# Attention in twelve batches of score chunks, and the root of the first norm in one turn

## The chip, the cores and the metric

The kernel runs on one core of a Trainium2 chip. The engines are TensorE (PE in the profile; PEld is its loading of weights), VectorE (DVE), ScalarE (ACT), GpSimd (POOL, unused here) and SyncE (SP), which issues nearly all transfers. The metric is the device time of one execution in microseconds (us), lower is better. Each engine executes its instructions in the order in which the program gives them, and waits on semaphores for the others.

## The reference

Three stages follow each other: attention with a sigmoid in place of the softmax (2 batches, 12 heads, 448 positions, 64 columns a head), a gated MLP with an RMS norm ahead of it (896 tokens, 768 to 1536 to 768), and an MLP with a SiLU (768 to 2048 to 768).

```python
scores = scale * np.matmul(q, k.transpose(0, 1, 3, 2)) - np.log(S)
attn = 1.0 / (1.0 + np.exp(-scores))
x = np.matmul(attn, v)          # then heads side by side: 896 x 768
rms = np.sqrt(np.mean(x * x, axis=-1, keepdims=True) + 1e-06)
xn = x / rms * rms_g
g = xn @ w_gate
x = (g * (1.0 / (1.0 + np.exp(-g))) * (xn @ w_val)) @ w_out
h = x @ w_in
return (h * (1.0 / (1.0 + np.exp(-h)))) @ w_out2
```

## The kernel before

**Pairs and chunks.** Attention works on 12 pairs of heads: pairs 0 to 5 are batch 0, pairs 6 to 11 batch 1. The 448 keys of a pair are three full chunks of 128 (c = 0, 1, 2) and a rest of 64. The rests of two neighbouring pairs, i and i + 1 with i even, form one chunk (i, 3), written (i, KC) in the code. So two pairs have seven chunks, and all have 42.

**Scores (`scores`, L403).** A full chunk is 6 matmuls in 64x128 tiles, for two heads side by side: k and q are split into a high part (fp32r) and a low rest, and three products are added. Their operand `ks` is made by `prep` on VectorE: a cast (L379) and a subtraction (L267); there are three buffers. A short chunk is 4 matmuls of unsplit fp32 in 64x64 tiles (8 records in the profile, since an fp32 matmul leaves two). Scores land in one of three PSUM tiles (`scp`, bufs=3), and ScalarE's sigmoid (L413) empties it into `a`.

**Attends (`attend`, L431).** A full chunk is 2 fp32 matmuls in 128x64 tiles (4 records), a short one 4 in 64x64 tiles (8 records), summed over a pair's chunks in a bank `av`, of which there are two (`avp`, bufs=2): pair 9 takes the bank of pair 7. `collect` copies a finished pair out of `av` into `xr` on VectorE (L448), which frees the bank. The square of the copy is made by ScalarE (L587), or, for pairs listed in `SQUARED`, by VectorE (L454); `add_square` adds it to the sum `acc` of its batch on VectorE (L467). The squares of pairs 7 to 10 share one buffer (tag s1, one deep).

**Turns.** `SIZES` cuts the list of chunks into batches. A turn issues the scores of one batch (full chunks first, the short one last) and then the attends of the batch before. When the scores of chunk (i, 0) are issued, `prep(i + 1)` and the loads of pair i + 3 are issued ahead of them. `PLAN` says what each turn issues at its end: `w` a step of the preparation of weights (merge of a slab, L288, casts, rests), `n` a step of `norm_first`; `EARLY` gives turn 9 one more `n` behind its scores.

**The norm of batch 0 (`norm_first`).** Its steps: split the sum of squares; two matmuls with ones that sum it over partitions (`ms0`, L472); first guess of the root (L482, L483) and a square on ScalarE (L486); a Newton step (L489, L490) and another square (L529); the last step (L493 to L495), which gives `r0`; then `normed`: for the x tiles in the order 0, 2, 4, 1, 3, 5, two at a time, scale on VectorE (L507), cast on ScalarE (L264, `high`) and rest on VectorE (L267, `low`). The first product behind attention (`g0`, L872) reads them in that order, six tiles and three matmuls each, of which the second needs the rest. The sums for batch 1 (into `v1_1`) and the product `g1` follow it; the banks for these overlay `av`, so `g1` also waits for the last `collect`.

**Behind attention** a planner (`Plan`) orders all work by fixed costs and due times. Those costs are not touched by the change.

Of the kernel before, what the change touches and what calls it, by code (L numbers as in the profile page):

```python
# [23 lines left out]
KC = S // P  # L24
# [3 lines left out]
HALF = 3 * P  # L28
NT = B * S
EPS = 1e-6  # L30
SIZES = [2, 2, 3] + [4, 3] * 5
DIRECT = ((0, 0),)
WOVEN = ((0, 1), (0, 2))
IDLE = 9
FIRST = (0, 1)
AFTER = {2: 1, 3: 1, 4: 2, 5: 4, 6: 4, 7: 5}
AWAY = (4,)
SQUARED = (5, 9)
ALIGNED = 4
LAG = {"A": 0.0481, "D": 0.081, "P": 0.165, "S": 4.4}  # L40
LOAD, LOAD_TILE = 2.8, 0.45
HOP = {"A": 0.516, "D": 0.3833, "S": 0.4}
# [10 lines left out]
LOADED = (6, 7)  # L53
LANDED = {7: 8.0}
LONG = 288
PLAN = ",,,www,wwwww,wwwww,wwww,wwww,nw,nn,n,wn,wnwn,w".split(",")
EARLY = {9: "n"}
LOADS = (0, 2)
RING = 9
# [5 lines left out]
class Job:  # L65


    def __init__(self, eng, cost, fn, deps, take, need):
# [3 lines left out]
        self.due, self.ready, self.left = 1e9, 0.0, 0  # L72
        self.lag = LAG[eng]
        for d in self.deps:
# [129 lines left out]
def tile_attention_two_mlps(  # L204
# [53 lines left out]
    def load_next():  # L258
        s = order.pop(0)
        place(s)  # L260
        load(s)
# [4 lines left out]
    def low(dst, src, hi):  # L266
        nc.vector.tensor_tensor(dst, src, hi.bitcast(F32), ALU.subtract)  # L267
# [60 lines left out]
    def step():  # L328
        do = next(steps, None)
        if do:  # L330
            do()
# [11 lines left out]
    with ExitStack() as actx:  # L343
# [9 lines left out]
        def pair_tile(i):  # L353
            kq[i] = ap.tile([P, 2, S], F32, tag="kq", name=f"kq{i}", bufs=6)

        def load_pair(i):
            b, hp = pairs[i]
            if i not in kq:
                pair_tile(i)
            if i:  # L360
                nc.sync.dma_start(kq[i], kqd[b, hp])
            else:
                nc.scalar.dma_start(kq[i][:, 1], kqd[b, hp, :, 1])
                for part in (slice(0, P), slice(P, S)):
                    nc.sync.dma_start(kq[i][:, 0, part], kqd[b, hp, :, 0, part])

        def load_v(i):
            vr[i] = ap.tile([P, KC + 1, 2, D], F32, tag="vr", name=f"vr{i}", bufs=5)
            n = KC if i % 2 else KC + 1
            if i == 0:  # L370
                nc.vector.memset(vr[i], 0.0)
            nc.sync.dma_start(vr[i][:, :n], vd[pairs[i]][:, :n])

        def prep(i):

            raw = kq[i]
            ks[i] = kst = ap.tile([P, 2, 2, S], F32R, tag="ks", name=f"ks{i}", bufs=3)
            if i:
                nc.vector.tensor_copy(kst[:, 0], raw)  # L379
                for part in (slice(0, 1), slice(1, 2)) if i == 1 else (slice(0, 2),):  # L380
                    low(kst[:, 1, part], raw[:, part], kst[:, 0, part])
            else:
                (hk, hq), (lk, lq) = ([kst[:, j, n] for n in range(2)] for j in range(2))
                tail = slice(P, S)
                nc.scalar.activation(hq, raw[:, 1], AF.Copy)
                nc.vector.tensor_copy(hk[:, tail], raw[:, 0, tail])
                low(lk[:, tail], raw[:, 0, tail], hk[:, tail])
                low(lq, raw[:, 1], hq)
# [27 lines left out]
        begun = {}  # L416

        def attend(i, c):

            a = att.pop((i, c))  # L420
            if c < KC:
                parts = [(i, slice(0, P))]
            else:
                parts = [(i + e, slice(e * KR, (e + 1) * KR)) for e in range(2)]
            for n, rows in parts:
                begun[n] = begun.get(n, 0) + 1
                if begun[n] == 1:
                    av[n] = avp.tile([P, 512], F32, tag="av", name=f"av{n}")
            for h in range(2):
                for n, rows in parts:  # L430
                    nc.tensor.matmul(  # L431
                        av[n][h * D : (h + 1) * D, :S],
                        vr[i][rows, c, h, :],
                        a[rows, h, :],
                        start=(begun[n] == 1),
                        stop=(begun[n] == KC + 1),
                        skip_group_check=True,
                    )
            return [n for n, rows in parts if begun[n] == KC + 1]

        def collect(i, copy_=True):

            b, hp = pairs[i]
            ps = av.pop(i)[:, :S]
            which, home_ = ("s1" if copy_ else "s3", sqs) if hp else ("s0", acc)
            xi = xr[hp // 2][:, b, hp % 2]
            if i < n - 2:
                nc.vector.tensor_copy(xi, ps)  # L448
            while added:
                add_square(added.pop(0))  # L450
            sq = home_[i if hp else b] = sp.tile([P, S], F32, tag=which, name=f"{which}{i}")
            if i < n - 2:
                if i in SQUARED:
                    nc.vector.tensor_tensor(sq, xi, xi, ALU.mult)  # L454
                else:
                    later.append((i, sq, xi))
            else:
                nc.scalar.activation(sq, ps, AF.Square)
                if copy_:
                    nc.vector.tensor_copy(xi, ps)  # L460
            return lambda: nc.vector.tensor_copy(xi, ps)

        def add_square(i):

            b, hp = pairs[i]
            if hp:
                nc.vector.tensor_tensor(acc[b], acc[b], sqs.pop(i), ALU.add)  # L467
# [6 lines left out]
        def split_sum(b, parts):  # L474

            high(parts[:, 0], acc[b])
            low(parts[:, 1], acc[b], parts[:, 0])
# [57 lines left out]
        n = len(pairs)  # L535
# [17 lines left out]
        load_v(2)  # L553
        nc.sync.dma_start(g_sb, gd)
        prep(0)
        turn_, ready, later, added, woven = 0, [], [], [], []
        chunks = []
        for i in range(0, n, 2):
            chunks += [(i, c) for c in range(KC + 1)] + [(i + 1, c) for c in range(KC)]
        batches = [[chunks.pop(0) for _ in range(n)] for n in SIZES]  # L560
        for before, batch in zip([[]] + batches, batches + [[]]):
            while len(ready) > 1:
                collect(ready[0])
                add_square(ready.pop(0))
            for i in ready:
                collect(i)
            for i, c in sorted(batch, key=lambda u: u[1] == KC):
                if c == 0:
                    if i + 1 < n:
                        prep(i + 1)  # L570
                    if i + 3 < n:
                        load_pair(i + 3)
                        load_v(i + 3)
                    if i in LOADS:
                        load_next()
                work = [scores(i, c)]
                if (i, c) in WOVEN:
                    woven += work
                    work = woven if len(woven) == len(WOVEN) else []
                for _ in zip(*work):  # L580
                    pass
                for rest in work:
                    for _ in rest:
                        pass
            while later:
                i, sq, xi = later.pop(0)
                nc.scalar.activation(sq, xi, AF.Square)  # L587
                added.append(i)
            while ready:
                i = ready.pop(0)  # L590
                if i not in added:
                    add_square(i)
            for what in EARLY.get(turn_, ""):
                next(normal, None)
            for i, c in sorted(before, key=lambda u: (max(0, u[0] // 2 - before[0][0] // 2), (u[1] != KC) == (turn_ < ALIGNED))):
                if ready and len(av) > 1 and any(n_ not in begun for n_ in ((i, i + 1) if c == KC else (i,))):
                    collect(ready[0])
                    add_square(ready.pop(0))
                ready += attend(i, c)
            final = [] if batch else [(i, collect(i, False)) for i in ready]  # L600
            if final:
                for i, _ in final:
                    add_square(i)
                next(normal, None)
                split_sum(1, squares)
                for _, copy_ in final:
                    copy_()
            for what in PLAN[turn_]:
                if what == "w":
                    step()  # L610
                else:
                    next(normal, None)
            turn_ += 1
# [19 lines left out]
    def dve(n, fn, deps=(), **more):  # L633
        return plan.add("D", 0.071 + n / 960, fn, deps, **more)
# [818 lines left out]
    for k in ORDER:  # L1453
# [5 lines left out]
        n_ = dve(1.13 * S, scale, [r_])  # L1459
# [95 lines left out]
    for t in range(3):  # L1555
        dest = lambda m, b, t=t: r2[t]()[:, b, m]
        n = 0 if t < 2 else 3
# [209 lines left out]
```

## Time and profile before

| what | us |
|---|---|
| median of 3 runs | 517.85 (517.82 to 518.41) |
| the profiled execution | 517.55 |
| its span in the profile | 515.8 |
| TensorE busy | 511.4 |
| VectorE busy | 457.6 |
| ScalarE busy | 388.6 |
| end of attention (first matmul of g0) | 69.4 from the start of the span |

The times in rows count from the start of the span. A row of the timeline merges instructions of one line that follow each other: start, length from the first start to the last end, engine, line, operation, tiles written and read, shape, count, and in brackets the idle time ahead and what ended it. Matmuls overlap, so a row on PE ends a little after the next has begun: the step from start to start tells what a block costs. A group by line gives the busy time and the mean of one in ns.

### The profile page before, as it was taken

The numbers are of one execution on the slowest core, as the hardware profiler recorded it, in microseconds if no ns is written. First come the engines' busy times: TensorE is split into PE (matmuls) and PEld (weight loads), VectorE is DVE, ScalarE is ACT, GpSimd is POOL, SyncE is SP. The second block draws the span as 40 slices with busy tenths as digits, with TensorE's granted clock in tenths as the row PEclk, the third lists the DMA queues.
The fourth block names the chain that finished last, engine by engine and source line by source line (L and its number), as shares of the span: only waits on it lengthen the run. The fifth ranks groups of instructions, "written<-read, shape, count | busy, mean of one in ns | idle before, by whom it ended". The sixth has DMA issues, their size and how long they took to land.

```text
span 515.8 us, 7423 instructions
## 1 busy us (share of the span) xinstructions
PE 511.4 (99%) x2648; PEld 442.7 (86%) x2648; DVE 457.6 (89%) x853; ACT 388.6 (75%) x701; POOL 0.2 (0%) x4
## 2 busy tenths in 40 slices
PE   9999999999999999999999999999999999999997
PEld 4544569999999999999999999999999999999996
DVE  5698999999998888699899989999977799999984
ACT  6898766588878787885578868899888798768430
POOL 0000000000000000000000000000000000000000
PEclk9999999999999999999999999999999999999999
DMA  8774110033434433330344350543552542626522
GB/s 300 261 278 174 61 58 4 1 122 124 131 133 172 173 128 123 122 124 0 124 159 167 102 180 8 180 136 116 187 185 102 174 145 91 227 111 220 183 109 72
DMA packets 20198, 70.48 MB, mean 137 GB/s; under 512 B 2369, under 2 KB 8257, under 8 KB 20161
## 3 DMA queue, kind: packets, MB, share of 16 engines
q1 hardware_dynamic: 19872, 69.69, 38.7%
q8 instruction: 21, 0.34, 0.3%
q10 hardware_dynamic: 288, 0.31, 0.2%
q14 instruction: 17, 0.13, 0.1%
HBM read 64.49 MB, written 5.51 MB: 136 GB/s over the span
## 4 chain that ended last, share of the span: by engine, by line
PE 99%; DVE 0%; DVEq 0%; issue 0%
PE av L431 7%; PE sc L403 6%; PE g L872 3%; PE v L872 3%; PE e2S L930 3%; PE e1x L930 2%; PE o2x L930 2%; PE e2a L930 2%; PE e0bx L930 2%; PE e0x L930 1%; PE o1x L930 1%; PE o0x L930 1%; PE e1y L930 1%; PE e1bx L930 1%; PE i6w L930 1%; PE i5w L930 1%
## 5 line engine op out<-in xcount | busy, mean ns | idle before, releaser
L288 DVE SCALAR_TENSOR_TENSOR f<-f,raw 128x768 uint32<-128x768 uint32 (+1 forms) x65 | 58.3, 899 | 9.1 <-ACT f L276 4.5
L264 ACT ACTIVATE w_S<-f 128x384 fp32r<-128x384 f32 (+1 forms) x90 | 43.5, 497 | 23.1 <-DVE f L792 8.1
L284 ACT ACTIVATE raw<-raw 128x768 int32<-128x768 uint32 (+1 forms) x70 | 57.0, 823 | 3.6 <-DMA raw<-in_w 3.6
L276 ACT ACTIVATE f<-raw 128x768 f32<-128x768 f32 (+1 forms) x65 | 55.4, 854 | 2.2 <-DVE w_S L267 1.8
L267 DVE TENSOR_TENSOR w_S<-f,w_S 128x384 fp32r<-128x384 f32 (+1 forms) x90 | 46.2, 524 | 4.7 <-ACT w_S L264 4.6
L267 DVE TENSOR_TENSOR w_A<-f,w_A 128x384 fp32r<-128x384 f32 (+1 forms) x84 | 44.6, 531 | 3.8 <-ACT w_A L264 3.7
L264 ACT ACTIVATE w_A<-f 128x384 fp32r<-128x384 f32 (+1 forms) x84 | 41.9, 500 | 4.9 <-PE o2y L872 2.0
L413 ACT ACTIVATE a<-sc,logs 128x896 f32<-128x896 f32 x42 | 39.1, 1010 | 7.9 <-PE sc L403 7.8
L431 PE MATMUL av<-a,vr 128*64 128x448 f32 (+1 forms) x192 | 35.3, 552 | 0.0
L431 PEld LDWEIGHTS av<-a,vr 128*64 128x64 f32 (+1 forms) x192 | 10.4, 135 | 21.3 <-issue 18.6
L403 PEld LDWEIGHTS sc<-ks 64*128 64x128 f32 x210 | 18.9, 185 | 9.5 <-ACT s L587 3.5
L403 PE MATMUL sc<-ks 64*128 64x448 f32 x210 | 24.9, 378 | 0.0
L1299 DVE TENSOR_TENSOR g<-g 128x448 f32<-128x448 f32 x32 | 19.4, 617 | 0.1
L264 ACT ACTIVATE w_S<-s 128x384 fp32r<-128x384 f32 x24 | 12.5, 521 | 8.9 <-DVE s L757 7.4
L872 PE MATMUL g<-x,w 128*128 128x448 f32 x72 | 15.2, 367 | 0.0
L264 ACT ACTIVATE w_S<-spare 128x128 fp32r<-128x128 f32 (+1 forms) x26 | 8.6, 329 | 8.6 <-DVE spare L839 2.9
L872 PEld LDWEIGHTS g<-x,w 128*128 128x128 f32 x72 | 13.5, 188 | 1.7 <-issue 0.7
L872 PE MATMUL v<-x,w 128*128 128x448 f32 x72 | 14.9, 365 | 0.0
L872 PEld LDWEIGHTS v<-x,w 128*128 128x128 f32 x72 | 13.5, 188 | 1.1
L267 DVE TENSOR_TENSOR w<-f,w 128x384 fp32r<-128x384 f32 (+1 forms) x22 | 9.8, 468 | 5.1 <-ACT w L264 5.1
L757 DVE TENSOR_TENSOR s<-f 128x384 f32<-128x384 f32 x24 | 13.3, 553 | 0.2
L267 DVE TENSOR_TENSOR ks<-kq,ks 128x896 fp32r<-128x896 f32 (+2 forms) x14 | 13.1, 948 | 0.4
(1441 smaller groups left out, 1473.8 us busy)
## 6 DMA issues: line engine op xcount, KB each, us to landing
raw<-in_w SPq DMA_DIRECT2D x52, 768.0 KB, 4.3
raw<-in_w SPq DMA_DIRECT2D x24, 512.0 KB, 3.7
kq<-in_kq SPq DMA_DIRECT2D x11, 448.0 KB, 5.2
out_t<-e SPq DMA_DIRECT2D x7, 224.0 KB, 1.9
vr<-in_v SPq DMA_DIRECT2D x6, 256.0 KB, 5.2
vr<-in_v SPq DMA_DIRECT2D x6, 192.0 KB, 5.1
g_4away<-g SPq DMA_DIRECT2D x4, 224.0 KB, 2.5
g<-g_4away SPq DMA_DIRECT2D x4, 224.0 KB, 5.6
```

Source lines behind the costliest of these rows:

```text
L264: nc.scalar.activation(dst, src, AF.Copy)
L267: nc.vector.tensor_tensor(dst, src, hi.bitcast(F32), ALU.subtract)
L276: nc.scalar.activation(floats[s], words(s)[:, :, 1].bitcast(F32), AF.Prelu, scale=2.0**-112, alpha=2.0**32)
L284: nc.scalar.activation(z.bitcast(I32), z, AF.Copy, scale=2.0**-29 * (1 - 2.0**-18), bias=-0.5 + 2.9e-5)
L288: nc.vector.scalar_tensor_tensor(fu, fu, 3, words(s)[:, :, 0], ALU.logical_shift_left, ALU.bitwise_or)
L403: nc.tensor.matmul(ps[to, h, :S], k_[:, keys], q_, start=(step == 0), stop=(step == 2 or plain), skip_group_check=True,)
L413: nc.scalar.activation(a, ps[:, :, :S], AF.Sigmoid, bias=logs, scale=D**-0.5)
L431: nc.tensor.matmul(av[n][h * D : (h + 1) * D, :S], vr[i][rows, c, h, :], a[rows, h, :], start=(begun[n] == 1), stop=(begun[n] == KC + 1), ...
L757: tt(sums[0], block(2), block(3), ALU.add)
L872: nc.tensor.matmul(banks[b](), t[:, jw], act[key](jx, b), start=(first and i == 0 and n_ == 0), stop=(final and i == n - 1 and n_ == 2), s ...
L930: nc.tensor.matmul(ps(), w[:, jw, j * P : (j + 1) * P], book[t][USES[a]][jx], start=(start and i == 0 and n == 0), stop=(stop and i == len ...
L1299: sub = lambda d, a, b: (lambda: tt(d(), a(), b(), ALU.subtract))
```

## The change

The batches become 2, 2, 3, eight times 4, and 3: twelve turns instead of thirteen, and four chunks in turns where three of them were full chunks and the fourth is now a full one of the next pair. Since a turn may now end within a pair, `prep(4)` is issued together with `prep(3)` (`AHEAD`), and loads are kept in `pending` until the pair five before has been attended. Pending sums of squares are added at the start of a turn. VectorE squares pair 8 instead of pair 9. In the turn whose earlier batch holds (8, KC), the short chunk is attended first, and pair 8 is collected right behind it (`EARLY_PAIR`). `PLAN` is moved to the new turns: the first guess, the Newton step and the last step of the root are all issued at the end of turn 9 (`nwnn`), where the last step was in turn 10 before.

```diff
-SIZES = [2, 2, 3] + [4, 3] * 5
+SIZES = [2, 2, 3] + [4] * 8 + [3]
-SQUARED = (5, 9)
+SQUARED = (5, 8)
+EARLY_PAIR = (8, KC)
+AHEAD = {2: (3, 4), 3: (), 11: ()}
-PLAN = ",,,www,wwwww,wwwww,wwww,wwww,nw,nn,n,wn,wnwn,w".split(",")
+PLAN = ",,,www,wwwww,wwwww,wwwww,wwww,n,nwnn,n,wnwn,w".split(",")
...
+        def load_pending():
+            while pending and (pending[0] < 5 or begun.get(pending[0] - 5) == KC + 1):
+                load_pair(pending[0])
+                load_v(pending.pop(0))
...
             for i in ready:
                 collect(i)
+            while added:
+                add_square(added.pop(0))
+            load_pending()
             for i, c in sorted(batch, key=lambda u: u[1] == KC):
                 if c == 0:
-                    if i + 1 < n:
-                        prep(i + 1)
+                    for n_ in AHEAD.get(i, (i + 1,)):
+                        prep(n_)
                     if i + 3 < n:
-                        load_pair(i + 3)
-                        load_v(i + 3)
+                        pending.append(i + 3)
+                        load_pending()
...
-            for i, c in sorted(before, key=lambda u: (max(0, u[0] // 2 - before[0][0] // 2), (u[1] != KC) == (turn_ < ALIGNED))):
+            for i, c in sorted(before, key=lambda u: (max(0, u[0] // 2 - before[0][0] // 2), (u[1] != KC) == (turn_ < ALIGNED or EARLY_PAIR in before))):
...
                 ready += attend(i, c)
+                if (i, c) == EARLY_PAIR:
+                    collect(ready[0])
+                    add_square(ready.pop(0))
```

TensorE, the turns around pairs 3 and 4, as it stands before (names are tile, pair and chunk; sc is scores, av attends; the last number only tells buffers apart):

```order
L403 MATMUL sc3_0_294<-ks3_231 128x448 x6
L403 MATMUL sc3_1_303<-ks3_231 128x448 x6
L403 MATMUL sc3_2_312<-ks3_231 128x448 x6
L431 MATMUL av2_322<-a2_0_246,vr2_136 64x448 x2
L431 MATMUL av2_322<-a2_1_255,vr2_136 64x448 x2
L431 MATMUL av2_322<-a2_2_264,vr2_136 64x448 x2
```

And the same place in the changed kernel:

```order
L405 MATMUL sc3_0_294<-ks3_231 128x448 x6
L405 MATMUL sc3_1_303<-ks3_231 128x448 x6
L405 MATMUL sc3_2_312<-ks3_231 128x448 x6
L405 MATMUL sc4_0_324<-ks4_234 128x448 x6
L433 MATMUL av2_334<-a2_0_249,vr2_136 64x448 x2
L433 MATMUL av2_334<-a2_1_258,vr2_136 64x448 x2
L433 MATMUL av2_334<-a2_2_267,vr2_136 64x448 x2
```

The first full chunk of pair 4 has moved into the block ahead of pair 2's attends, as a fourth full chunk.

VectorE, from the first guess of the root to its last step, as it stands before (ms, r0 and t0 are the root's tiles, xr takes a pair out of av, ks is a prep, f4 a merge of weights):

```order
L482 TENSOR_SCALAR ms_635<-ms0_626 128x448
L483 TENSOR_SCALAR r0_636<-ms_635 128x448
L489 SCALAR_TENSOR_TENSOR t0_637<-t0_637,ms_635 128x448
L490 SCALAR_TENSOR_TENSOR r0_636<-t0_637,r0_636 128x448
L529 TENSOR_TENSOR t0_637<-r0_636 128x448
L448 COPY xr0_90<-av7_573 128x448
L379 CAST ks10_646<-kq10_534 128x896
L267 TENSOR_TENSOR ks10_646<-kq10_534,ks10_646 128x896
L493 SCALAR_TENSOR_TENSOR t0_637<-t0_637,ms_635 128x448
L494 SCALAR_TENSOR_TENSOR t0_637<-t0_637 128x448
L495 SCALAR_TENSOR_TENSOR r0_636<-t0_637,r0_636 128x448
```

And in the changed kernel:

```order
L484 TENSOR_SCALAR ms_672<-ms0_660 128x448
L485 TENSOR_SCALAR r0_673<-ms_672 128x448
L290 SCALAR_TENSOR_TENSOR f4_551<-f4_551,raw_79 128x768
L491 SCALAR_TENSOR_TENSOR t0_674<-t0_674,ms_672 128x448
L492 SCALAR_TENSOR_TENSOR r0_673<-t0_674,r0_673 128x448
L531 TENSOR_TENSOR t0_674<-r0_673 128x448
L495 SCALAR_TENSOR_TENSOR t0_674<-t0_674,ms_672 128x448
L496 SCALAR_TENSOR_TENSOR t0_674<-t0_674 128x448
L497 SCALAR_TENSOR_TENSOR r0_673<-t0_674,r0_673 128x448
L450 COPY xr0_90<-av7_604 128x448
```

The copy of av7 and the prep of pair 10 stood between the Newton step and the last step; now the copy stands behind the whole root, and the prep ahead of it.

ScalarE, from the casts of x0 and x2 to that of x4, as it stands before (s18 and s19 are squares of pairs 8 and 9, a11 the sigmoids of pair 11):

```order
L587 ACTIVATE s18_694<-xr1_91 128x448
L264 ACTIVATE x0_84<-xr0_90 128x448
L264 ACTIVATE x2_86<-xr1_91 128x448
L413 ACTIVATE a11_0_756<-sc11_0_749,logs_82 128x896
L413 ACTIVATE a11_1_765<-sc11_1_758,logs_82 128x896
L413 ACTIVATE a11_2_774<-sc11_2_767,logs_82 128x896
L276 ACTIVATE f5_789<-raw_79 128x768
L264 ACTIVATE x4_88<-xr2_92 128x448
```

And in the changed kernel:

```order
L266 ACTIVATE x0_84<-xr0_90 128x448
L266 ACTIVATE x2_86<-xr1_91 128x448
L415 ACTIVATE a11_0_755<-sc11_0_748,logs_82 128x896
L415 ACTIVATE a11_1_764<-sc11_1_757,logs_82 128x896
L415 ACTIVATE a11_2_773<-sc11_2_766,logs_82 128x896
L598 ACTIVATE s19_747<-xr1_91 128x448
L278 ACTIVATE f5_788<-raw_79 128x768
L266 ACTIVATE x4_88<-xr2_92 128x448
```

The square of pair 8 has left ScalarE, and that of pair 9 has come in behind the sigmoids of pair 11, ahead of the cast of x4.

## Rows read from the trace of the kernel before

**Rows 1.** The page's first part: busy us, share of the span, instructions.

```profile
PE 511.4 (99%) x2648; PEld 442.7 (86%) x2648; DVE 457.6 (89%) x853; ACT 388.6 (75%) x701; POOL 0.2 (0%) x4
```

**Rows 2.** Timeline of TensorE in attention: start, length, line, tiles, count.

```profile
7.37 1.72 PE L431 MATMUL av<-a,vr 128*64 128x448 f32 x8
9.02 2.12 PE L403 MATMUL sc<-ks 64*128 64x448 f32 x18
...
18.25 2.09 PE L403 MATMUL sc<-ks 64*128 64x448 f32 x18
20.27 3.39 PE L431 MATMUL av<-a,vr 128*64 128x448 f32 x20
23.59 2.09 PE L403 MATMUL sc<-ks 64*128 64x448 f32 x18
25.61 0.98 PE L403 MATMUL sc<-kq 64*64 64x448 f32 x8
26.52 2.48 PE L431 MATMUL av<-a,vr 128*64 128x448 f32 x12
28.93 2.09 PE L403 MATMUL sc<-ks 64*128 64x448 f32 x18
...
48.01 0.68 PE L472 MATMUL ms<-two,x 128*128 128x448 f32 x2
```

**Rows 3.** Timeline of all engines from 14 to 45 us, four rows.

```profile
18.25 1.72 PEld L403 LDWEIGHTS sc<-ks 64*128 64x128 f32 x18 [0.70 <-ACT s L587]
...
24.50 3.70 ACT L413 ACTIVATE a<-sc,logs 128x896 f32<-128x896 f32 x4 [0.40 <-PE sc L403]
...
33.45 1.09 DVE L267 TENSOR_TENSOR ks<-kq,ks 128x896 fp32r<-128x896 f32 x1
...
34.27 2.22 PE L403 MATMUL sc<-ks 64*128 64x448 f32 x18
```

**Rows 4.** Timeline of all engines around the end of attention, six rows.

```profile
62.62 2.80 ACT L413 ACTIVATE a<-sc,logs 128x896 f32<-128x896 f32 x3 [0.24 <-PE sc L403]
...
66.11 1.06 ACT L264 ACTIVATE x<-xr 128x448 fp32r<-128x448 f32 x2
...
69.45 3.92 PE L872 MATMUL g<-x,w 128*128 128x448 f32 x18
...
71.00 1.15 DVE L267 TENSOR_TENSOR x<-xr,x 128x448 fp32r<-128x448 f32 x2
...
72.61 0.62 DVE L461 COPY xr<-av 128x448 f32<-128x448 f32 x1
...
73.61 1.58 PE L872 MATMUL g<-x,w 128*128 128x448 f32 x7
```

**Rows 5.** The page's fifth part, the group of the sigmoids.

```profile
L413 ACT ACTIVATE a<-sc,logs 128x896 f32<-128x896 f32 x42 | 39.1, 1010 | 7.9 <-PE sc L403 7.8
```

**Rows 6.** Timeline of VectorE from 44 to 76 us, steps of the root.

```profile
48.94 0.62 DVE L482 TENSOR_SCALAR ms<-ms 128x448 f32<-128x448 f32 x1
...
50.65 0.63 DVE L489 SCALAR_TENSOR_TENSOR t<-t,ms 128x448 f32<-128x448 f32 x1 [0.67 <-ACT t L486]
51.31 0.62 DVE L490 SCALAR_TENSOR_TENSOR r<-t,r 128x448 f32<-128x448 f32 x1
...
56.02 0.62 DVE L495 SCALAR_TENSOR_TENSOR r<-t,r 128x448 f32<-128x448 f32 x1
56.56 0.61 DVE L448 COPY xr<-av 128x448 f32<-128x448 f32 x1
```

**Rows 7.** Groups of VectorE by line and shape, 4 to 72 us.

```profile
L267 DVE TENSOR_TENSOR ks<-kq,ks 128x896 fp32r<-128x896 f32 x10 | 10.9, 1093 | 0.3
...
L448 DVE COPY xr<-av 128x448 f32<-128x448 f32 x10 | 6.2, 618 | 3.4 <-PE av L431 3.4
...
L288 DVE SCALAR_TENSOR_TENSOR f<-f,raw 128x768 uint32<-128x768 uint32 x5 | 4.8, 956 | 3.0 <-ACT f L276 3.0
...
L507 DVE SCALAR_TENSOR_TENSOR xr<-xr,g_sb,r 128x448 f32<-128x448 f32 x6 | 3.8, 671 | 0.0
```

More of the change, by code (lines that the diff above doesn't have):

```diff
@@ L555, in tile_attention_two_mlps @@
         prep(0)
-        turn_, ready, later, added, woven = 0, [], [], [], []
+        turn_, ready, later, added, woven, pending = 0, [], [], [], [], []
+        def load_pending():
+            while pending and (pending[0] < 5 or begun.get(pending[0] - 5) == KC + 1):
+                load_pair(pending[0])
+                load_v(pending.pop(0))
         chunks = []
```

## The prediction

> **What bounds the kernel now.** Read the page's first part first: TensorE is busy 511.4 of 515.8 us, VectorE 89%, ScalarE 75% [rows 1]. In the timeline of TensorE through attention each row begins where the one ahead of it is about to end [rows 2], so the time there is the sum of the blocks on TensorE, plus what a block waits for. Four kinds of block alternate. I call them S (scores of full chunks, 6 records each), R (scores of a short chunk, 8 records), A (attends of full chunks, 4 records each) and B (attends of a short chunk, 8 records). From start to start [rows 2]: S of three chunks 20.27 - 18.25 = 2.02, R 26.52 - 25.61 = 0.91, A of three chunks 28.93 - 26.52 = 2.41, A of three with B 23.59 - 20.27 = 3.32, so B is 0.91. One block is held visibly: the S at 34.27 takes 2.22 instead of 2.09, because VectorE's low halves of that pair's k and q end at 33.45 + 1.09 = 34.54 [rows 3]. So a hold of some 0.03 cost 0.13, of which 0.1 is the restart of the stream. The rest of attention has no hold, and neither has the start of the first product, the first 18 matmuls of which take 3.92 us [rows 4]. But that product lives on what VectorE and ScalarE finish just before, and this decides the change.
>
> **Part 1: fewer blocks (gain).** The number of matmuls is the same, only the block boundaries go. The A at 7.37 has 8 records (4 pairs side by side), the one at 26.52 has 12 (6 pairs), so a pair costs (2.41 - (9.02 - 7.37)) / 2 = 0.38 [rows 2], a chunk 0.75, and the boundary of an A of three 2.41 - 6 x 0.38 = 0.13 to 0.16. The 18 weight loads of an S take 1.72, two side by side, or 0.19 to 0.20 a pair [rows 3]; the boundary of an S is then 2.02 - 9 x 0.2 = 0.22 (0.31 at 0.19). The order shows one S and one A less, and one place (the turn of 10_0 to 10_3) where R is followed directly by B in the same 64x64 tiles, which saves about one more boundary of 0.15. Sum 0.5 to 0.6; I take 0.55. The held S at 34.27 is not the same block any more: 0.13 more.
> [...]
>
> **Part 2: four full chunks in one S (loss, three times).** Three turns now write the scores of four full chunks into three PSUM tiles. The fourth must wait for the sigmoid of the first. In the turn at 23.59 the first sigmoid starts at 24.50 [rows 3], one takes 1.01 [rows 5], so it ends 1.92 after the block began, and a matmul behind it can start at 1.97 to 2.02 (R started at 2.02). Unhindered, the fourth chunk would start some 0.1 earlier than that R, at 1.91, since there is no boundary ahead of it. A hold of 0.06 to 0.11 and the restart of 0.1: 0.15 each, 0.45 in all, bounds 0 (no hold) and 2.0 (ScalarE late, rival b). Parts 1 and 2 together: -0.55 - 0.13 + 0.45 = about -0.2. The prep of pair 4 that moves ahead one turn (1.7 us on VectorE) and the loads that are put off behind free buffers I cost at nothing: of all the preps only the one at 33.45 held TensorE [rows 3], and pair 4 is needed one turn after its prep. If the cover fails, it is a hold like that at 34.27, of 0.1 to 0.5.
>
> **Part 3: the root in one turn.** This decides. The sum of squares (ms0) is at 48.01 now [rows 2]. In the new order it stands behind S and R of the turn of 9_0 to 9_2 and 8_3. Walk from the S at 18.25, which stays: five turns alternate between 2.62 + 0.15 + 3.32 = 6.09 (S of four, A, B) and 2.02 + 0.91 + 2.41 + 0.75 = 6.09 (S, R, A of four), so the S of 9 starts at 18.25 + 5 x 6.09 = 48.7, and ms0 at 48.7 + 2.93 = 51.6, that is 3.6 us later, while the end of attention without a hold would come at 51.6 + 0.6 + 3.15 (A of four) + 2.02 + 1.67 (R with B) + 2.41 + 5.34 + 2.41 = 69.2 against 69.45 now [rows 4]. So the norm has 17.6 us where it had 21.4.
> VectorE can start when ms0 ends, 51.6 + 0.68 + 0.04 = 52.3. From the first step to the first Newton step 50.65 - 48.94 = 1.71 pass [rows 6] (a merge of a weight slab, 0.96 [rows 7], now stands in between and mostly fits into the wait for ScalarE's square): 54.05; I take 54.2, since ScalarE's queue has the fourth sigmoid and a square ahead. Then six dependent steps at 51.31 - 50.65 = 0.66 [rows 6]: 58.2, against 56.02 + 0.62 = 56.64 now. In the old order the copies of av7 and the prep of pair 10 stood between them and went first; in the new one the whole root stands ahead of the copy of av7 (0.62 [rows 7]), which ends at 58.75.
> Hold 1: there are two av tiles, and av9 takes av7's. TensorE reaches the B of 8_3, which begins av9, at 51.6 + 0.6 + 3.15 + 2.02 + 0.81 = 58.2. It is held until 58.8: 0.6, and 0.1 for the restart.
> Behind the copy, VectorE goes on without a gap, with the durations of [rows 7] (cast, adds and squares like the copy, all of 448 columns a half). A step that needs the one ahead of it starts 0.03 after its end (51.31 against 50.65 + 0.63), one that does not 0.08 before it (56.56 against 56.02 + 0.62) [rows 6]: prep of pair 11 (0.65 + 1.01), copy of av8 0.53, add 0.65, square of pair 8 (now VectorE's) 0.66, add 0.53, scale 0.68: from 58.63 to 63.35. ScalarE's queue has the casts of x0 and x2 ahead of the sigmoids of pair 11. Those could start at 63.1, but the casts wait for the scales, so they start at 64.45. From there to the end of the casts of x4 and x1 it is 66.11 + 1.06 - 62.62 = 4.55 now [rows 4], and the square of pair 9 (now ScalarE's) adds some 0.5, like one cast of 1.06 for two: 69.45. VectorE, done with its earlier work at 67.2, waits for these casts: x1's low half 69.5 to 70.1, then two scales and only then the add of pair 9's square, until 71.85. ScalarE's square of pair 10 needs that add, because both squares use one buffer (tag s1): 71.9. Behind it in ScalarE's queue, x3's cast comes at 72.75. On VectorE copy of av10, two adds, the low halves of x3 and x5 follow: 72.45 + 0.53 + 0.65 + 0.53 + 1.15 = 75.3. Now they end at 71.00 + 1.15 = 72.15 [rows 4].
> Hold 2: the matmul that needs x5's low half is the 17th of the first product, 16 x (73.61 - 69.45) / 20 = 3.3 behind its start [rows 4] (18 matmuls and 2 of the sums until 73.61): at 72.8 now, so the margin is 0.6. Without holds it would be wanted at 72.55; it comes at 75.35. After it, the last copy (av11, 72.61 + 0.62 = 73.23 now) ends at 76.4, and g1, which needs its bank, starts there instead of at 73.61: 2.8 later, with the restart 2.9. Every walk with shortest spacings comes out early: the steps from 56.64 to 73.23 walked in the old order give some 0.2 less than the rows show. I add that: +3.1. Behind g1 the orders are the same, and TensorE has no hold in what follows, so nothing gives it back.
> Sum: the profiled execution took 517.55 us (span 515.8 and 1.75 around it): 517.55 + 3.1 = 520.65. The median of the runs, 517.85, lies 0.3 above it: 520.95, and I say 521.0.
>
> **The rivals.** (a) The gain alone: the norm is hidden as it is now. For it speaks that VectorE and ScalarE each have idle time in attention (ScalarE 7.9 us waiting for scores [rows 5]) and that the margin of x5 is 0.6. It decides if the low half of x5 comes by 72.6, that is 2.7 us earlier than by my walk; then 517.85 - 0.2 = 517.6, or 517.2 if the fourth chunks are not held either. Against it speaks that the walk has no step that could be left out.
> (b) Sigmoids late. In three turns a late ScalarE now holds TensorE, where it did not before, since only S blocks of three were without a fourth chunk. It decides where ScalarE is busy when the first chunk's scores end; with a cast of 0.5 in the way (1.06 for two [rows 4]) 3 x 0.5 = 1.5 more: 522.5.
> [...]
> (c) A third hold: VectorE stays behind after g1, and the product with the second half of the batch, which follows g1 and its two sister products, is late. The first holds give VectorE just as much time, so it should not be; with 1 us more 522.0.
> (d) Half of it: the holds are shorter, by a walk that is wrong in one queue place (the square of pair 10 not behind the add): x3 and x5 come 1.2 sooner, 519.8.
>
> **Chances.** Forecast 0.73 (520.3 to 521.8), (a) 0.09, (b) 0.08, (c) 0.05, (d) 0.05. The range 519.4 to 522.6 leaves out (a) and parts of (b). About 0.2% (1.04 us) is what a measurement of this kernel can tell from no change. (a) lies within it, as the boundaries give 0.7 at most; faster than that needs something that I don't see: 0.02. Same 0.08, slower 0.90.
>
> **What would show it.** In the timeline after: S blocks of 24 records at 2.7 instead of 2.6; ms0 at 51.5 to 51.8; a pause of about 0.6 ahead of the 64x64 attends near 58; VectorE idle near 67 to 69 until ScalarE's cast of x4; the first g product at 6 us or more instead of 3.92; and from g1 on the same spacing as before. If the root's last step ends before 57, or g keeps its 3.92, the walk is wrong.

## The result and the profile after

The changed kernel is slower. The median of its six executions is 522.5 us, and 522.1 over the four that the ratio compares, against 518.13 for the kernel before in the same comparison: a ratio of 1.0076, interval [1.0061, 1.0091]. A second comparison, with more executions of the kernel before, gave 1.0083 [1.0068, 1.0098]. The prediction was 521.0, with a chance of 0.73 for 520.3 to 521.8 and a range of 519.4 to 522.6: the change goes the way that was forecast, and the time lies in the range but above what I held most likely. The ratios leave disturbed executions out; the profiled one of the changed kernel is such a one (531.11 us; behind the pauses shown below, from about 80 us on, its matmuls stand 0.207 apart instead of 0.203), as are some of the profiled ones of the experiments, so I read these traces only up to there.

By the mean granted clock of TensorE (1.000 is full speed throughout), the seven executions compared in the two comparisons fall into two groups: 521.58, 521.73 and 521.89 us at a clock of 1.000, and 522.21 to 522.71 at 0.995 to 0.999. So some 3.7 us are one matter, and some 0.8 more in most executions may be another.

The timeline of TensorE after the change (start, length, line, tiles, count, and in brackets the idle time ahead and what ended it):

```profile
9.13 2.09 PE L405 MATMUL sc<-ks 64*128 64x448 f32 x18
...
18.33 2.91 PE L405 MATMUL sc<-ks 64*128 64x448 f32 x24
21.17 3.39 PE L433 MATMUL av<-a,vr 128*64 128x448 f32 x20
...
30.60 2.85 PE L405 MATMUL sc<-ks 64*128 64x448 f32 x24
33.38 3.39 PE L433 MATMUL av<-a,vr 128*64 128x448 f32 x20
...
51.83 0.68 PE L474 MATMUL ms<-two,x 128*128 128x448 f32 x2
...
58.45 3.92 PE L433 MATMUL av<-a,vr 64*64 64x448 f32 x20
...
64.31 5.79 PE L433 MATMUL av<-a,vr 128*64 128x448 f32 x32
70.03 2.70 PE L886 MATMUL g<-x,w 128*128 128x448 f32 x12
73.74 0.48 PE L886 MATMUL g<-x,w 128*128 128x448 f32 x1 [1.00 <-ACT x L266]
75.29 1.68 PE L886 MATMUL g<-x,w 128*128 128x448 f32 x5 [1.08 <-DVE x L269]
...
77.51 4.72 PE L886 MATMUL g<-x,w 128*128 128x448 f32 x18
```

Against [rows 2] and [rows 4]: S blocks of 24 records exist now, 2.78 to 2.84 from start to start. ms0 is 3.8 us later. The first product, one block of 3.92 before, is in three pieces with two pauses, ahead of x3's first matmul, the 13th (it waits for ScalarE's cast), and of x3's second (VectorE's low half). The second product (g1) starts at 77.51 instead of 73.61, and takes 4.72, though it has as many matmuls as the first, which took 3.92 [rows 4].

What the pauses wait for, on ScalarE and VectorE (same columns):

```profile
63.61 1.18 ACT L266 ACTIVATE x<-xr 128x448 fp32r<-128x448 f32 x2 [2.92 <-DVE xr L509]
64.69 2.79 ACT L415 ACTIVATE a<-sc,logs 128x896 f32<-128x896 f32 x3
67.36 0.58 ACT L598 ACTIVATE s<-xr 128x448 f32<-128x448 f32 x1
67.82 0.92 ACT L278 ACTIVATE f<-raw 128x768 f32<-128x768 f32 x1
68.64 1.04 ACT L266 ACTIVATE x<-xr 128x448 fp32r<-128x448 f32 x2
72.24 0.98 ACT L460 ACTIVATE s<-av 128x448 f32<-128x448 f32 x2 [2.57 <-DVE s L469]
73.11 1.04 ACT L266 ACTIVATE x<-xr 128x448 fp32r<-128x448 f32 x2
```

```profile
57.77 0.63 DVE L497 SCALAR_TENSOR_TENSOR r<-t,r 128x448 f32<-128x448 f32 x1
58.31 0.62 DVE L450 COPY xr<-av 128x448 f32<-128x448 f32 x1
...
62.90 1.27 DVE L509 SCALAR_TENSOR_TENSOR xr<-xr,g_sb,r 128x448 f32<-128x448 f32 x2
...
69.24 1.16 DVE L269 TENSOR_TENSOR x<-xr,x 128x448 fp32r<-128x448 f32 x2 [1.80 <-ACT x L266]
70.32 1.27 DVE L509 SCALAR_TENSOR_TENSOR xr<-xr,g_sb,r 128x448 f32<-128x448 f32 x2
71.51 0.62 DVE L469 TENSOR_TENSOR s<-s,s 128x448 f32<-128x448 f32 x1
72.82 0.62 DVE L462 COPY xr<-av 128x448 f32<-128x448 f32 x1 [0.69 <-ACT s L460]
73.36 1.35 DVE L469 TENSOR_TENSOR s<-s,s 128x448 f32<-128x448 f32 x2
74.62 1.16 DVE L269 TENSOR_TENSOR x<-xr,x 128x448 fp32r<-128x448 f32 x2
...
76.23 0.62 DVE L463 COPY xr<-av 128x448 f32<-128x448 f32 x1
```

Read it as a relay. ScalarE waits 2.92 for the first scales, then does pair 11's sigmoids, pair 9's square (67.36) and a weight slab, and only then the casts of x4 and x1 (68.64). VectorE waits 1.80 for these. Its scales and the add of pair 9's square follow (71.51), ScalarE has waited 2.57 for that add, and so x3 and x5 come at 74 to 76. Both engines that are "late" are idle for part of the time: in this trace neither is short of capacity, each waits for the other.

### The profile page after: what moved, and what is told of

It reads as the page before. It is cut to its first block, busy times and chain, and to the rows that moved or that the text cites. A ratio compares the mean times of both kernels' runs of the same rounds, so it can differ in the third digit from the quotient of the medians.

```text
span 529.2 us, 7431 instructions
## 1 busy us (share of the span) xinstructions
PE 522.7 (99%) x2648; PEld 443.5 (84%) x2648; DVE 459.5 (87%) x853; ACT 388.8 (73%) x701; POOL 0.2 (0%) x4
## 4 chain that ended last, share of the span: by engine, by line
PE 95%; DVE 3%; ACT 1%; issue 0%; DVEq 0%; ACTq 0%
PE sc L405 5%; PE av L433 4%; PE e2S L944 3%; PE v L886 3%; PE g L886 3%; PE e1x L944 2%; PE e0bx L944 2%; PE e2a L944 2%; PE o2x L944 2%; PE e0x L944 1%; PE o1x L944 1%; PE o0x L944 1%; PE e1y L944 1%; PE e1bx L944 1%; PE i7w L944 1%; PE i6w L944 1%
## 5 line engine op out<-in xcount | busy, mean ns | idle before, releaser
L886 PE MATMUL g<-x,w 128*128 128x448 f32 x72 | 17.2, 392 | 2.1 <-DVE x L269 1.1
```

The lines of the kernel that those rows point to most:

```text
L886: nc.tensor.matmul(banks[b](), t[:, jw], act[key](jx, b), start=(first and i == 0 and n_ == 0), stop=(final and i == n - 1 and n_ == 2), s ...
```

## The experiments

Two theories stood against each other. **Theory 1** is what my prediction put first: ms0 and the root are late and the root is one unbroken piece on VectorE. **Theory 2** came from reading the idle times above: the order of the last turns, with the scales of x0 and x2 behind the copy of av8 and the squares, and the square of pair 9 on ScalarE with its add behind further scales.

**The changed kernel again.**

> The changed kernel once more, for a trace to read the others against. Expected 521.5 to 522.5 us: the first product at about 64.4 and 5.8 us long, two pauses in it of about 0.9 each ahead of the matmuls of x3 and x5. If TensorE's granted clock is below full speed in some stretch, it should be right behind those two pauses (76 to 79 us); if the drop has another cause, it stands elsewhere.

Measured: 521.89 to 522.71 us, ratio 1.0083 [1.0068, 1.0098]. The trace can't serve for what it was meant for: its execution took 720.90 us, with a mean granted clock of 0.659, low nearly from the start to the end (0.74 in the first 20 us, 0.65 in every stretch from 20 to 600), so no fall behind the two pauses can be looked for in it. What follows is read against the trace above.

**The root's steps left out.**

```diff
-            newton()
-            nc.vector.tensor_tensor(t, r, r, ALU.mult)
             yield
-            third()
             yield
```

> The changed kernel with the six Newton steps of the first norm's root left out (the output is then not the reference's). VectorE has 6 x 0.66 = 3.9 us less to do ahead of the copy of av7. Theory 1, as in my prediction (the length of the root in one turn decides): hold 1 goes, and all that follows on VectorE comes up to 3 us earlier, so 518.3 to 519 us, 3 below the changed kernel. Theory 2 (the order of the last turns decides: the scales stand behind the copy of av8 and the adds of two squares, which come when TensorE and ScalarE deliver, and the square of pair 9 and its add stand behind the scales): only hold 1 goes, and most of it comes back as a longer wait in the first product; 521 to 521.3 us, 0.4 to 0.7 below, with VectorE idle before 62 us and the scales of x0 still near 62.

Measured: 521.39 and 521.40 us, ratio 1.0066 [1.0049, 1.0084]. VectorE's timeline and the start of the first product in TensorE's:

```profile
59.55 0.62 DVE L450 COPY xr<-av 128x448 f32<-128x448 f32 x1 [2.75 <-PE av L433]
60.84 0.63 DVE L469 TENSOR_TENSOR s<-s,s 128x448 f32<-128x448 f32 x1 [0.66 <-ACT s L595]
...
62.70 1.27 DVE L509 SCALAR_TENSOR_TENSOR xr<-xr,g_sb,r 128x448 f32<-128x448 f32 x2
```

```profile
58.57 3.34 PE L433 MATMUL av<-a,vr 64*64 64x448 f32 x20
...
69.58 2.70 PE L883 MATMUL g<-x,w 128*128 128x448 f32 x12
73.55 0.47 PE L883 MATMUL g<-x,w 128*128 128x448 f32 x1 [1.27 <-ACT x L266]
```

Hold 1, the wait of TensorE's 64x64 attends for the bank of pair 7, is gone (3.34 instead of 3.92), and VectorE now stands idle for 2.75 waiting for av8, and 0.66 for a square of ScalarE's. The scales start at 62.70 instead of 62.90: with 3.9 us of work taken away ahead of them they come 0.2 sooner. The first pause grows by 0.27 and eats half of hold 1. By the ratios the gain is 0.9 us, with intervals that overlap, and against the changed kernel's executions at a clock of 1.000 it is 0.3 (both executions here are at 0.998). Theory 1, which asked for 3, falls.

**The norm's start moved up, root and all.** Two small tables say behind which scores and attends a step of the norm is issued: "a" adds the waiting square (pair 5's), "n" does the norm's next step. ms0 comes to stand behind the attends of pair 7's second chunk.

```diff
-PLAN = ...,n,nwnn,n,wnwn,w
-EARLY = {9: "n"}
+AFTER_S = {(7, 2): "a", (8, 1): "n"}
+AFTER_A = {(7, 1): "n"}
+PLAN = ...,n,nwn,n,wnwn,w
+EARLY = {}
...
```

> The changed kernel with only the norm's start moved: the sum of squares behind the attends of pair 7's second chunk, some 3.4 us earlier, and the root's steps with it; the square of pair 9 and the place of the scales as in the changed kernel. The lateness of ms0 and of the root, which my prediction put first: if it is what costs, 518 to 518.6 us. Theory 2: the scales, behind the copy of av8 and the adds, do not move, so only hold 1 goes and comes back as a longer first product: 521.2 to 521.6 us.

Measured: 521.55 to 522.41 us, ratio 1.0081 [1.0060, 1.0101]. The timelines of TensorE and of VectorE: ms0 is at 47.99 in this trace and the root's last step ends at 56.69, but the scales are still late:

```profile
47.99 0.85 PE L477 MATMUL ms<-two,x 128*128 128x448 f32 x2
...
73.57 0.47 PE L899 MATMUL g<-x,w 128*128 128x448 f32 x1 [1.26 <-ACT x L269]
```

```profile
56.07 0.62 DVE L500 SCALAR_TENSOR_TENSOR r<-t,r 128x448 f32<-128x448 f32 x1
...
62.74 1.27 DVE L512 SCALAR_TENSOR_TENSOR xr<-xr,g_sb,r 128x448 f32<-128x448 f32 x2
```

Six microseconds pass between the finished root and its first use. An early norm alone is worth nothing that can be measured (1.0081 against 1.0083).

**The root in one turn, alone, in the kernel before.**

```diff
-PLAN = ",,,www,wwwww,wwwww,wwww,wwww,nw,nn,n,wn,wnwn,w".split(",")
+PLAN = ",,,www,wwwww,wwwww,wwww,wwww,nw,nnn,,wn,wnwn,w".split(",")
```

> The kernel before with only the plan of the root changed: the steps of the turn behind go into the turn of the sum's, all else (thirteen batches, squares, order of preps) as before. Theory 1: a root in one turn stands ahead of a copy or a prep in any order, and costs 1 us or more here: 518.8 to 519.5. Theory 2: in this order the norm has 21 us and the root is hidden but for a prep behind it: a hold of 0.2 to 0.3 at the scores of pair 10, 518.0 to 518.4, same as before.

Measured: ratio 1.0004 [0.9996, 1.0013], 518.12 us median: no difference. The hold is there and is as small as theory 2 had it; this is the S of pair 10 in its timeline, 2.36 where an unhindered one has 2.09:

```profile
56.25 2.36 PE L403 MATMUL sc<-ks 64*128 64x448 f32 x18
```

**The root split again, in the changed kernel.**

```diff
-PLAN = ...,n,nwnn,n,wnwn,w
+PLAN = ...,n,nwn,nn,wnwn,w
```

> The changed kernel with the root's last two steps back in the turn behind, as before the change, so that the copy of av7 and the prep of pair 11 go first. Theory 1 (root in one turn is what costs): hold 1 goes, so 520.9 us or less. Theory 2 (what costs is that the root, the scales and the last squares all stand late in the order): hold 1 goes, but the scales move back by a copy, a prep of 1.65 us and more, so that the sigmoids of pair 11 are later still; 522.8 to 523.5 us, with a hold ahead of the last attends.

Measured: 524.10 to 525.27 us, ratio 1.0122 [1.0106, 1.0137]: slower than the changed kernel by about 0.4%, and by more than theory 2 had worked out (522.8 to 523.5). In the timelines of VectorE and of TensorE the scales start 1.7 later, and the first pause is 2.54 instead of 1.00:

```profile
64.58 1.28 DVE L509 SCALAR_TENSOR_TENSOR xr<-xr,g_sb,r 128x448 f32<-128x448 f32 x2
```

```profile
75.41 0.65 PE L886 MATMUL g<-x,w 128*128 128x448 f32 x1 [2.54 <-ACT x L266]
```

So in this order of batches the root in one turn is not the fault; it is the better of the two.

**The square of pair 9 on VectorE.**

```diff
-SQUARED = (5, 8)
+SQUARED = (5, 8, 9)
```

> The changed kernel with one number more: the square of pair 9 on VectorE again instead of ScalarE, where it stood behind pair 11's sigmoids and ahead of the casts of x4 and x1. Theory 2 (the order of the last turns): casts of x4 and x1 0.5 earlier, and the square of pair 10 no longer behind an add that stands behind two scales: 1.2 to 1.7 us gained, 520 to 520.4. Theory 1 (the root's length): VectorE, already late, has 0.65 more to do, so no gain, 521.5 to 522.5.

Measured: 519.94 us (519.69 to 520.17), ratio 1.0039 [1.0025, 1.0054]. One pause is left of the two, in TensorE's timeline:

```profile
70.44 2.90 PE L886 MATMUL g<-x,w 128*128 128x448 f32 x13
73.90 1.28 PE L886 MATMUL g<-x,w 128*128 128x448 f32 x5 [0.56 <-DVE x L269]
```

More work for VectorE, less time for the kernel: about 1.7 us of the 3.7, by one number. This is what theory 2 says and theory 1 excludes. Two things change at once, and the time doesn't part them: set against the start of the first product, which is 0.41 later here, ScalarE's casts of x4 and x1 come 0.5 earlier (68.56), and its square of pair 10, which no longer waits for an add, 3.1 earlier (69.50).

**The scales one place earlier.**

```diff
-PLAN = ...,n,nwnn,n,wnwn,w
-EARLY = {9: "n"}
+PLAN = ...,n,nwnn,,wnwn,w
+EARLY = {9: "n", 10: "n"}
```

> The changed kernel with the scales of x0 and x2 issued one place earlier: on VectorE they stand ahead of the copy of av8, the adds of two squares and the square of pair 8, instead of behind them. Theory 2 (the order of the last turns): ScalarE's casts of x0 and x2, and the sigmoids of pair 11 behind them, no longer wait for av8, so they come some 1.3 earlier and x3 and x5 with them: 520.2 to 520.6 us. Theory 1 (the root's length decides): the scales still follow the root at once, only the copy of av8 moves back behind them, and the time stays at 521.5 or gets longer.

Measured: 520.49 to 520.97 us, ratio 1.0048 [1.0030, 1.0066]: about 1.2 gained, as expected. In the timelines of ScalarE and of VectorE, pair 11's sigmoids now wait only for TensorE's scores, and the wait for the cast of x4 shrinks from 1.80 to 0.38:

```profile
63.90 2.80 ACT L415 ACTIVATE a<-sc,logs 128x896 f32<-128x896 f32 x3 [0.83 <-PE sc L405]
```

```profile
68.50 1.16 DVE L269 TENSOR_TENSOR x<-xr,x 128x448 fp32r<-128x448 f32 x2 [0.38 <-ACT x L266]
```

**Both of these.**

> The changed kernel with the square of pair 9 on VectorE and the scales of x0 and x2 one place earlier, both, but ms0 where the changed kernel has it. The two gains measured apart are about 1.6 to 1.7 and 1.0 us. If they are independent, 518.8 to 519.1 us. If they overlap (with either alone out of the way, VectorE itself is the next late one, since it does root, prep and squares without a gap from ms0 on), 519.8 to 520.1, as with the square alone; only an earlier ms0 with both then gives the rest.

Measured: 519.32 us (519.08 to 519.65), ratio 1.0028 [1.0016, 1.0039]. Between the two expectations: of 1.7 + 1.2, some 2.2 arrive. Now VectorE has no idle time from 53.3 to the copy of av11 at 74.16, and in TensorE's timeline x3's low half is still 0.44 late:

```profile
73.23 1.28 PE L886 MATMUL g<-x,w 128*128 128x448 f32 x5 [0.44 <-DVE x L269]
```

With the queue places mended, VectorE itself is the late one, and a late ms0 and a long root may have a price of their own; the next run tells.

**All three: an earlier ms0, the scales, the square.** The edits of the three experiments on ms0, scales and square together (ms0 behind the attends of pair 7's second chunk, `SQUARED = (5, 8, 9)`, `EARLY = {10: "n"}`), with the twelve batches kept.

> The twelve batches kept, the norm woven in earlier: the square of pair 5 is added behind pair 7's third chunk of scores and its sum split at once, ms0 stands behind the attends of pair 7's second chunk instead of behind the scores of 9_2, the square of pair 9 is VectorE's, and the scales of x0 and x2 stand ahead of the copy of av8. Both holds should go, so that what is left is parts 1 and 2 of my prediction. By my prediction 517.6 us (-0.55 for the boundaries, +0.45 for three holds of the fourth chunk of scores, -0.13). By what the trace of the changed kernel shows of the scores of four chunks (start to start 2.78 to 2.84 instead of 2.62, three times, so +0.55 in all) and with -0.55 and a small hold around ms0: 517.9 to 518.4, no difference from the kernel before. The granted clock should be 1.00 throughout.

Measured: 518.10 us (517.57 to 520.23), against 518.20 for the kernel before: ratio 0.9999 [0.9988, 1.0009]. The first product is one block again in TensorE's timeline:

```profile
9.71 2.12 PE L408 MATMUL sc<-ks 64*128 64x448 f32 x18
...
48.59 0.85 PE L477 MATMUL ms<-two,x 128*128 128x448 f32 x2
...
70.20 3.91 PE L899 MATMUL g<-x,w 128*128 128x448 f32 x18
```

The whole loss is undone, to within the half microsecond of the interval, so it was in the order of the norm's steps and the squares, and the twelve batches themselves are worth nothing that can be measured. Moving ms0 and the root up, worth nothing alone, is worth 0.0028 + 0.0001 = 0.29%, or 1.5 us, once the two queue places are mended. How much of it is ms0 and how much the root behind it was not parted. From the first S of three to the first product it is 70.20 - 9.71 = 60.49, against 69.45 - 9.02 = 60.43 before [rows 2, 4]. No version tried beats the kernel before.

**The pauses filled.** Five matmuls whose result nothing reads ahead of x3's first matmul in the first product, and five ahead of its second:

```diff
+FILL = {(4, 0): 5, (4, 1): 5}
...
+                    for _ in range(FILL.get((i, n_), 0) if fill else 0):
+                        nc.tensor.matmul(fill, t[:, 0], act["x", 0](0, 0), start=True, stop=True, skip_group_check=True)
```

> The changed kernel with ten matmuls more, whose result nothing reads: five of x0 into the bank of a later product right ahead of the first matmul of x3 in the first product, and five ahead of its second, so that TensorE works through most of the two pauses (1.17 and 1.35 us from the end of one matmul to the start of the next; five take 1.0). If the pauses themselves were all that costs, the time stays at 521.5 to 521.9. If the fall of the granted clock to 0.50 from 76 to 79.4 us comes of the two pauses, it does not appear here: granted clock 1.00 from 64 to 84 us, matmuls behind x5 at 0.20 us each, all runs near 521.6 and none at 522.5. If it comes of something else (a state of the chip, the load on other engines), it appears as in the changed kernel.

Measured: 521.26 us (520.72 to 521.76), ratio 1.0058 [1.0046, 1.0071], all executions at a granted clock of 1.000. Table of TensorE in stretches (stretch, its length, busy time and matmuls, granted clock, DMA share, GB/s), first of the changed kernel, then of this one:

```profile
72.00:76.00 4.00, 1.92 (x8) 1.00 0.00 0
76.00:79.40 3.40, 3.40 (x11) 0.50 0.19 43
```

```profile
72.00:76.00 4.00, 3.92 (x18) 1.00 0.00 0
76.00:79.40 3.40, 3.40 (x17) 1.00 0.17 40
```

And the timeline of TensorE with the pauses filled:

```profile
73.76 0.47 PE L889 MATMUL g<-x,w 128*128 128x448 f32 x1
...
75.32 1.29 PE L889 MATMUL g<-x,w 128*128 128x448 f32 x5
...
76.92 3.31 PE L889 MATMUL g<-x,w 128*128 128x448 f32 x15
```

(The last row is cut off at 80 us.) x3's matmuls stand where they stood (73.76 and 75.32, against 73.74 and 75.29), so nothing that TensorE waits for has moved. The fall of the clock is gone: g1 starts at 76.92 instead of 77.51, and what follows it, at 82.07 there, comes here, by my estimate, at about 80.7 (76.92 and the 3.75 that g1 takes with the square on VectorE, 75.50 to 79.25), some 1.4 earlier. By the ratios the kernel with ten matmuls more is faster by 0.18 to 0.25% (1.0058 against 1.0076 and 1.0083), or 0.9 to 1.3 us; the intervals overlap, so the size is rough, but all five executions lie below the four of the changed kernel with a mean clock under 1.000.

All of it in one table: the excess over the kernel before in the same comparison (ratio less 1, times 518), each known to some 0.5 to 1.0 us by its interval.

| Kernel | Excess, us |
|---|---|
| changed kernel, second comparison (first; its executions at clock 1.000) | 4.3 (3.9; 3.7) |
| root's steps left out | 3.4 |
| norm's start moved up | 4.2 |
| root in one turn, in the kernel before | 0.2 |
| root split again | 6.3 |
| square on VectorE | 2.0 |
| scales earlier | 2.5 |
| square and scales | 1.5 |
| square, scales and earlier ms0 | -0.1 |
| pauses filled | 3.0 |

## Why the prediction was right, and where it was wrong

**The sign and the place were right.** The steps of the walk, predicted and in the trace: ms0 51.6 and 51.83; end of the root 58.2 and 58.40; sigmoids of pair 11 64.45 and 64.69; end of the casts of x4 and x1 69.45 and 69.68; square of pair 10 71.9 and 72.24; low half of x5 75.35 and 75.78; end of the last copy 76.4 and 76.85. Each is late by 0.2 to 0.45, about the 0.2 that I added for too short spacings. Hold 1 was 0.58 for 0.6 to 0.7. VectorE's wait for the cast of x4 was there as named, and the first product was broken, but not where I had it: I put hold 2 at the 17th matmul, which needs x5's low half, and TensorE was held at the 13th and 14th, which need x3's cast and its low half; the end of the product and the last copy, from which the sum was taken, are the same.

**Parts 1 and 2 were right.** From the S of three at 9.13 to the first product at 70.03 it is 60.90; without hold 1 60.32, against 60.43 before [rows 2, 4]: -0.11, where I had about -0.2. The hold at a fourth chunk is 0.16 to 0.22 (2.78 to 2.84 against the 2.62 of my walk), not 0.15, or 0.55 in all, which leaves -0.66 for part 1, where I had -0.68. So rival (b) is out, though its 522.5 is the time that was measured: the fourth chunk waits for the first sigmoid three times, but with its restart that costs a fifth of a microsecond each. The 0.15 that part 1 gave to the place where R is followed by B was an estimate; with the root left out, where hold 1 is gone, R, B and an A of three take 61.83 - 57.76 = 4.07 from start to start, against 0.91 + 3.32 = 4.23 for R and for A with B before [rows 2], so 0.16.

**The cause named in part 3 was wrong.** "The root in one turn. This decides" is the step that failed, and with it, in rival (a), "the walk has no step that could be left out": the six steps of the root are 3.9 us of that walk, and leaving them out gave 0.3 of 3.7 or, counted with the clock, 0.9 of 4.3. The root in one turn alone costs nothing in the old order (1.0004), and splitting it again in the new one costs more (1.0122). What failed was the method: I walked forward, each step behind the one ahead of it, and took the first late one for the cause. VectorE's queue had a wait for av8 and for ScalarE's square behind the copy of av7, both ending 1 us or less before the walk got there (copy of av8 and add at 59.55 and 60.84 with the root left out, at 60.51 and 61.04 with it); with the root shorter they end last. The sum came right all the same, because such a walk takes the later side at each wait; it doesn't tell which earlier step, if shortened, brings anything. The links that do count were in the walk as well, but as details: the scales behind the copy of av8, the square of pair 9 ahead of ScalarE's casts, and its add behind two scales. Mended alone, the square gives 3.7 - 2.0 = 1.7 and the scales' place 1.2, both 2.2, and with ms0 and the root moved up as well all of it. So the late norm that part 3 named has a share after all, 1.5 us, but only behind these two. Rival (d), the square of pair 10 not behind the add, was put at 519.8; the kernel that makes it so took 519.94.

**The term that was missing is the clock.** The sum had no line for it. The mechanism without it is the kernel with the pauses filled: ratio 1.0058, 3.1 us over the kernel before in the same comparison (521.26 against 518.20), which is the +3.1 of the sum. The rest of the changed kernel's 3.9 to 4.3 us is, as far as the runs show, the fall of the clock and what it drags behind: 0.9 to 1.3 us between the two kernels, and 0.8 us between the changed kernel's own executions at a clock of 1.000 and those below. Why its executions at 1.000 still stand 0.6 above the filled kernel is not settled; that is within the spread of single executions, and a mean over 520 us to three places would hide a fall of half a microsecond. So 521.0 was about the right sum of what it counted, and the time came out above the 521.8 of my forecast by what it did not count.

## What to carry to other kernels

When a walk through the queues ends in a late step, walk back from it and ask at each wait which of its two sides ended last, and by how much; a long step that is followed by an idle engine is not yet the cause, and the cheapest proof is a run with that step left out. Causes can also hide each other: here the early norm gained nothing until two queue places were mended, and then 1.5 us. Where two engines hand work back and forth, the queue place of one small operation (here a square of 0.6 us) can be worth more than the length of any. Pauses of TensorE should be priced with the clock behind them: here the changed kernel lost 0.9 to 1.3 us against the one with its two pauses filled.

## What the runs showed of the hardware

In the changed kernel's trace TensorE's granted clock fell from 1.00 to 0.50 of full speed behind two pauses with a wait of 1.00 and 1.08 and one matmul between them (72.6 to 75.3 us), although in the 60 us before it had been held only by the 0.6 of hold 1 near 58.8 and by a fifth of a microsecond at each of the three fourth chunks. It stood at 0.50 from 76.00 to 79.40, during which TensorE was busy throughout, and the matmuls came 0.373 apart instead of 0.203. The other kernels with two such pauses show the same. In the table of stretches, first the one with the root's steps left out, then the one with the norm's start moved up (clock 0.62 and 0.57, of which 3.4 us at 0.50, from 75.6 and from 76.3):

```profile
76.00:80.00 4.00, 4.00 (x14) 0.62 0.34 97
```

```profile
76.00:80.00 4.00, 4.00 (x14) 0.57 0.32 97
```

The one with the root split, whose pauses are 2.54 and 0.90, stands at 0.50 from 75.5 to 82.3. The traces with a single pause (0.56, 0.91 and 0.44) show 1.00 around it, and so does the one with the two filled.

The mean clocks of the other executions agree. A fall like that of the changed kernel's trace takes 0.003 off the mean (0.5 x 3.4 of 529 us; the trace's mean is 0.997). Of 24 executions of the four kernels with two pauses (leaving out the one at 0.659), 16 have a mean of 0.997 or less; of 83 of the kernel before and of the six others, none is below 0.998. A mean of 0.999 alone doesn't show such a fall: the trace of the square and scales (0.999) has a clock of 1.00 from 40 to 300 us. In the trace of the kernel before (mean 1.000) the clock falls to 0.50 only behind the last instruction, which ends at 515.8: it is 0.50 from 516.5 to 517.0 and 1.00 again from 518. The three executions of the kernel before at 0.998 (518.53, 518.65 and 518.71 us) have no trace; without such a pause they need not have had a fall within the work.

The fall doesn't always come: three of the changed kernel's executions had a mean clock of 1.000. What else decides it was not tried, nor whether one pause of 1.0 or two shorter ones would do it, since the single pauses here are all under 1.0.
